# Joining attention's product with v into the scores' step, planning by a ring of four PSUM buffers, and dealing the weight preparation anew, in a kernel of attention and two MLPs

## The chip, the cores and the metric

The kernel runs on one core of a Trainium2 chip. The metric is the device time of one execution in microseconds (us).

## The reference

```python
def sm_attn(qq, kk, vv):
    s = scale * np.matmul(qq, kk.transpose(0, 1, 3, 2))
    s = s - np.max(s, axis=-1, keepdims=True)
    a = np.exp(s)
    a = a / (np.sum(a, axis=-1, keepdims=True) + 1e-09)
    return np.matmul(a, vv)
p_packed = sm_attn(p, k, v)            # 32 rows of p for each of 8 x 8 heads; q, k, v: 576 x 64 a head
out = sm_attn(q, p_packed, p_packed)
x = out.transpose(0, 2, 1, 3).reshape(4608, 512)
h = x @ w_in;   x = (h * sigmoid(h)) @ w_out              # MLP 1: 512 -> 2048 -> 512
h = x @ w_in2;  out = (h * clip(h + 3, 0, 6) / 6) @ w_out2   # MLP 2, the same sizes
```

All is fp32. The kernel gets its precision on TensorE (PE) by splitting each operand into a high and a low part (gh and gl, for example) and multiplying three times.

## The kernel before

**Blocks.** The 4608 rows of x are dealt into nine blocks of 512. Block j (0 to 7) holds the first 512 positions of batch j, block 8 the last 64 positions of all. MLP 1 runs over the blocks in order. A block goes through 16 slices f of the 2048 hidden units: `hidden` (L899 to L901) puts a 128 x 512 tile hps into PSUM, ACT takes silu of it (L907) and the high part gh (L914), DVE the low part gl (L915), and `project` (L922 to L924) multiplies it into four accumulators acc two slices later. In blocks 1 to 7 attention's second product is folded into MLP 1: packed values times w_in (`fuse_steps`, L660 to L662, written M here) give the tiles named fused, xf, xh, xl or raw, which `hidden` multiplies with the attention weights a2h and a2l; a slice then has 6 matmuls for hidden (written H) and 12 for project (P), against 12 and 12 in blocks 0 and 8. From about 823 us on the second MLP runs, which the change does not touch.

**Attention between the matmuls.** Heads come in groups of four, numbered n = 0 to 15 (two for each batch). Blocks 0 to 6 carry the attention of later blocks as short interruptions of PE's stream. One window of attention works on three groups at once: the first softmax of one (c, p against k), the second of another (d, q against the packed values), and what follows for two earlier ones (b and a). Its steps are

- `step_kpq` (L404 to L413): transposes of group b's softmax weights (d in the trace; ACT copies them into a T buffer at L108, DVE copies the tail a1Tt at L111), of p, and of the 64-position tails kt and qt;
- `step_tr` (L432 to L438): transposes of q and k rows into T buffers, by PE and ACT for n below 4, by DVE alone (L438) from n = 4 on;
- `products_pp` (L464, L467): group b's weights times v, the packed values; then pt (L486) and xt (L596), two single transposes;
- `step_zs` (L506 to L519): the scores of d (z) and c (s), each a 512-wide bank, and one bank `rest` for all 64-wide tails;
- `exps`: the exponentials on ACT (L449, L548), each with a change of the activation table before it and another for the silu behind it; `ends`: row sums and the division on DVE (L454, L455, L554 to L557).

All of these, and the M products, take their PSUM from one pool of four buffers (abank); hps comes from another tag of the same kind. A buffer that is asked for while its last reader has not finished stops PE.

**What sets the order.** The program of each engine is fixed in advance by `Plan`. Its clock `now` counts 512-wide matmuls. A step stands in a list with a place in the block, a cost, the steps that it needs, and a wait in matmuls after each of them, from the table WAIT (FIRST in block 0); it runs at the first `tick` at which its place is reached, its waits are over, a T buffer is free (`held`, four of them) and, if it asks for PSUM, its entry of `banks` (two release times) has passed. `exps` runs only right behind a slice's gh and gl.

**Loads.** `use` hands out the loads of later groups on SP's queue: tails of v and q, two v pieces, eight q and eight k pieces for a group from n = 4 on (L356, L366, L373).

**Preparation.** `Prep` turns the second MLP's weights into seven pieces in two precisions: 32 units of nine steps (two loads praw, conversions on ACT at L180, L186, L332 and L333, on DVE and on GpSimd, three stores). `nxt` calls `prep.step` once a slice in blocks 1 to 6, three times in block 7 and four times in block 8 after the first slices. In block 8 the second MLP's first x pieces are loaded as well.

## Time and profile before

| | us |
|---|---|
| median of 3 runs (1526.87 to 1527.33) | 1526.9 |
| the profiled execution | 1522.9 |
| its span | 1521.0 |
| PE busy in it | 1481.4 |
| block 0 begins | 35.7 |
| blocks 1, 2, 3, 4 begin | 151.2, 251.1, 340.4, 418.6 |
| blocks 5, 6, 7, 8 begin | 506.0, 588.1, 667.1, 732.6 |
| second MLP begins | 823.0 |

The profile has a row for each instruction: engine, line, operation, output and input tile, start and duration, and the idle time before it with the engine or transfer that ended it. The views used below are the page's busy times, the waits of one engine summed by who released them, the timeline of one engine, and windows (busy time of every engine, granted clock of PE and DMA rate in a stretch).

### The profile page before, as it was taken

To read this page: it belongs to the slowest core of one execution; us is meant where nothing else is said; L and a number is where in the kernel's file an instruction comes from. 1 tells how busy PE (TensorE), PEld (TensorE's weight loads), DVE (VectorE), ACT (ScalarE), POOL (GpSimd) and SP (SyncE) were. 2 spreads that over 40 slices of the span, in tenths; PEclk is the share of its full clock that TensorE was granted. 3 is DMA by queue.
4 is the path that set the end of the run, shared out by engine and by line. 5 is a ranking of instruction groups with operands and counts; after the bars stand their busy time and mean duration, and the time that the engine had idled before them with its cause. 6 is when DMAs were issued, how large, how long until landed. Compare 5 with 4: busy or idle time off the path is not lost.

```text
span 1521.0 us, 21714 instructions
## 1 busy us (share of the span) xinstructions
PE 1481.4 (97%) x7550; PEld 1227.8 (81%) x7550; DVE 1038.6 (68%) x1695; ACT 779.7 (51%) x1241; POOL 193.8 (13%) x177
## 2 busy tenths in 40 slices
PE   7999998999999999999999999999999999999998
PEld 4767766777777777788878888888888888999998
DVE  6767466655676556753543769776978687778777
ACT  6876656555666456564443344433443344444443
POOL 2433112111211211122231000000000000000000
PEclk9999999999999999999999999999999999999999
DMA  9998789897798768868696667577767766898987
GB/s 247 313 319 266 231 235 266 243 237 193 187 253 231 201 169 271 234 177 224 216 303 202 193 214 226 193 221 241 225 195 220 237 219 209 285 314 252 276 271 221
DMA packets 434508, 358.51 MB, mean 236 GB/s; under 512 B 191200, under 2 KB 325856, under 8 KB 434400
## 3 DMA queue, kind: packets, MB, share of 16 engines
q1 hardware_dynamic: 423632, 343.79, 77.3%
q10 hardware_dynamic: 10768, 13.34, 2.7%
q8 instruction: 61, 1.00, 0.3%
q14 instruction: 47, 0.39, 0.1%
HBM read 295.17 MB, written 61.87 MB: 235 GB/s over the span
## 4 chain that ended last, share of the span: by engine, by line
PE 83%; DVE 4%; ACT 4%; DMA 3%; SPq 2%; issue 1%; POOL 1%; ACTq 0%; DVEq 0%; POOLq 0%
PE b L1174 8%; PE b L1175 8%; PE b L1173 8%; PE b L1268 8%; PE b L1271 7%; PE b L1270 7%; PE acc L922 7%; PE acc L923 7%; PE acc L924 7%; PE hps L899 4%; PE hps L901 4%; PE hps L900 4%; SPq L373 1%; DMA w1i<-win 1%; PE abank L660 1%
## 5 line engine op out<-in xcount | busy, mean ns | idle before, releaser
L915 DVE TENSOR_TENSOR gl<-hps,gh 128x512 fp32r<-128x512 f32 x144 | 98.8, 686 | 157.6 <-ACT gh L914 157.1
L1270 PE MATMUL b<-ro,ws 128*128 128x512 f32 (+2 forms) x564 | 206.3, 366 | 0.0
L1271 PE MATMUL b<-ro,ws 128*128 128x512 f32 (+2 forms) x564 | 206.2, 366 | 0.0
L1173 PE MATMUL b<-xc,ws 128*128 128x512 f32 (+1 forms) x560 | 205.6, 367 | 0.0
L1175 PE MATMUL b<-xc,ws 128*128 128x512 f32 (+1 forms) x560 | 205.6, 367 | 0.0
L1174 PE MATMUL b<-xc,ws 128*128 128x512 f32 (+1 forms) x560 | 205.6, 367 | 0.0
L1216 DVE TENSOR_TENSOR ro<-g,ro 128x1024 fp32r<-128x1024 f32 (+1 forms) x140 | 161.1, 1155 | 42.3 <-ACT ro L1211 41.9
L1211 ACT CAST ro<-g 128x1024 fp32r<-128x1024 f32 (+1 forms) x140 | 132.1, 967 | 93.9 <-DVE g L1204 33.3
L1268 PE MATMUL b<-ro,ws 128*128 128x512 f32 (+2 forms) x564 | 139.0, 367 | 0.3
L907 ACT ACTIVATE hps<-hps 128x512 f32<-128x512 f32 x144 | 84.2, 585 | 86.4 <-PE hps L901 85.6
L922 PE MATMUL acc<-gh,wr 128*128 128x512 f32 x288 | 115.7, 402 | 1.7 <-ACT gh L914 1.7
L1270 PEld LDWEIGHTS b<-ro,ws 128*128 128x128 f32 x564 | 105.9, 188 | 13.2
L1271 PEld LDWEIGHTS b<-ro,ws 128*128 128x128 f32 x564 | 105.9, 188 | 13.1
L1173 PEld LDWEIGHTS b<-xc,ws 128*128 128x128 f32 x560 | 105.1, 188 | 13.3
L1174 PEld LDWEIGHTS b<-xc,ws 128*128 128x128 f32 x560 | 105.1, 188 | 13.2
L1175 PEld LDWEIGHTS b<-xc,ws 128*128 128x128 f32 x560 | 105.1, 188 | 12.9
L1268 PEld LDWEIGHTS b<-ro,ws 128*128 128x128 f32 x564 | 102.9, 188 | 15.0 <-DVE ro L1216 2.1
L922 PE MATMUL acc<-gh,wo 128*128 128x512 f32 x288 | 114.4, 397 | 0.0
L923 PE MATMUL acc<-gl,wr 128*128 128x512 f32 x288 | 113.4, 394 | 0.2 <-DVE gl L915 0.2
L924 PE MATMUL acc<-gh,wr 128*128 128x512 f32 x288 | 113.1, 393 | 0.0
L923 PE MATMUL acc<-gl,wo 128*128 128x512 f32 x288 | 112.4, 390 | 0.5 <-DVE gl L915 0.5
L924 PE MATMUL acc<-gh,wo 128*128 128x512 f32 x288 | 112.4, 390 | 0.0
(310 smaller groups left out, 2892.6 us busy)
## 6 DMA issues: line engine op xcount, KB each, us to landing
ws<-w2in SPq DMA_DIRECT2D x280, 256.0 KB, 3.4
ws<-w2out SPq DMA_DIRECT2D x280, 256.0 KB, 3.4
wi<-w1i SPq DMA_DIRECT2D x80, 512.0 KB, 5.9
wo<-w1o SPq DMA_DIRECT2D x64, 512.0 KB, 5.8
x1d<-x SPq DMA_DIRECT2D x18, 512.0 KB, 5.6
w1i<-win SPq DMA_DIRECT2D x16, 512.0 KB, 7.4
praw<-in_moe_w_in_dram SPq DMA_DIRECT2D x32, 256.0 KB, 5.8
praw<-in_moe_w_out_dram SPq DMA_DIRECT2D x32, 256.0 KB, 6.2
```

The lines of the kernel that those rows point to most:

```text
L915: nc.vector.tensor_sub(out=gl, in0=g, in1=f32(gh))
L922: mm(acc[e], lhsT=w[:, 0, s], rhs=gh, start=first, stop=False)
L923: mm(acc[e], lhsT=w[:, 0, s], rhs=gl, start=False, stop=False)
L924: mm(acc[e], lhsT=w[:, 1, s], rhs=gh, start=False, stop=last)
L1173: mm(ps, lhsT=wh, rhs=xs[k][:, 0, c], start=first, stop=False, skip_group_check=True)
L1174: mm(ps, lhsT=wh, rhs=xs[k][:, 1, c], start=False, stop=False, skip_group_check=True)
L1175: mm(ps, lhsT=wl, rhs=xs[k][:, 0, c], start=False, stop=last, skip_group_check=True)
L1211: nc.scalar.copy(out=t[:, 0], in_=v)
L1216: nc.vector.tensor_sub(out=t[:, 1], in0=self.operand(s), in1=f32(t[:, 0]))
L1268: mm(to, lhsT=wh, rhs=x, start=False, stop=last, skip_group_check=True)
L1270: mm(to, lhsT=wh, rhs=x, start=first, stop=False, skip_group_check=True)
L1271: mm(to, lhsT=wl, rhs=x, start=False, stop=False, skip_group_check=True)
```

## The change

1. From block 2 on, `products_pp` of group b and the transposes pt and xt are done inside `step_zs`, in free columns of its bank `rest`; pt and xt of a group that just finished go into the next `step_kpq` (arguments p and x). Block 1 keeps `products_pp` as a step of its own.
2. `Plan` keeps four release times (`ring`) in place of two, puts `hidden`'s tile into it as well, and asks that the next one does not come free later than the next hidden tile will want it. M products hold 15 in place of 11, T buffers are five in place of four, and the table of waits is different, with one for block 1 (SECOND): the exponentials wait longer after the scores, and the transposes longer after the exponentials. The transposes of k and q (`turn`) no longer stand behind `step_kpq` and pp.
3. `Prep`'s scratch buffer pr is one in place of two; block 7 does five steps a slice (78 in all, 46 before), block 8 two (32, 62 before). The loads of the second MLP's first x pieces go out one at a time in place of eight together.

The matmuls themselves are the same: PE has 6164 rows of instructions in place of 6165.

```diff
-            return self.pool.tile([P, T], F32, tag="pring", name="pr", bufs=2)
+            return self.pool.tile([P, T], F32, tag="pring", name="pr")
...
-    def step_kpq(c, d, b):
+    def step_kpq(c, d, b, p=None, x=None):
...
+        if p is not None:
+            step_pt(p)
+        if x is not None:
+            step_xt(x, ps[:, 3 * P:])
...
-            st["a1", b] = half_kb(b, "T", 4)
+            st["a1", b] = half_kb(b, "T", 5)
...
-    def products_pp(n):
+    def products_pp(n, ps=None):
         vm, vt = [nat.pop(("v", n, j)) for j in range(2)], nat.pop(("v", n))
         a, at_ = st.pop(("a1", n)), st.pop(("a1t", n))
-        ps = bank()
+        ps = bank() if ps is None else ps
...
-    def step_zs(c, d, b, a):
+    def step_zs(c, d, b, a, p=None):
...
         if b is not None:
-            step_pt(b, rest[:, P:2 * P])
+            products_pp(b, rest[:, 2 * TAIL:3 * TAIL])
+        if p is not None:
+            step_pt(p, rest[:, 3 * TAIL:5 * TAIL])
         if a is not None:
-            step_xt(a, rest[:, 2 * P:3 * P])
+            step_xt(a, rest[:, 5 * TAIL:7 * TAIL])
         if d is not None:
...
         if b is not None:
-            step_ptc(b)
+            st["pp", b] = value_pp(b, rest[:, 2 * TAIL:3 * TAIL])
+        if p is not None:
+            step_ptc(p)
...
-            self.steps, self.open, self.done, self.tiles, self.banks = [], set(), {}, [], [0, 0]
+            self.steps, self.open, self.done, self.tiles, self.ring = [], set(), {}, [], [0] * 4
+            self.hidden = self.period = 0
...
-            return tile and len(self.tiles) > 3 and self.tiles[-4] in self.open
+            return tile and len(self.tiles) > 4 and self.tiles[-5] in self.open
+
+        def take(self, hold):
+            self.ring = self.ring[1:] + [max(self.now, self.late) + hold * self.slow]
...
-            if bank and self.banks[count == 3] > self.now:
+            if bank and (max(self.ring[:count]) > self.now or self.slow > 1 and self.ring[count] > max(self.now, self.hidden + self.period)):
...
-                self.banks = [self.banks[1], max(self.now, self.late) + bank * self.slow]
+                self.take(bank)
...
+        def turn():
+            add(d, "q0", 0, lambda: step_tr(d, "q", 0), bank=0, tile=("z", d))
+            add(d, "q1", 0, lambda: [step_tr(d, "q", 1), use("q", d)], ("q0", d), bank=0, tile=("z", d))
+            add(a, "u", 0, lambda: [step_u(a), step_ut(a)], before[1], bank=8)
+            add(c, "k0", 0, lambda: step_tr(c, "k", 0), (("q1", d), 0), bank=0, tile=("s", c))
+            add(c, "k1", 0, lambda: [step_tr(c, "k", 1), use("k", c)], ("k0", c), bank=0, tile=("s", c))
...
+            p = pend.pop() if pend else None
+            p0, p1 = (p, None) if p is not None and p == d else (None, p)
...
+            def transposes():
+                step_kpq(c, d, b, p0, x)
...
+                add(keys[0][1], keys[0][0], 2 * n_banks, transposes, before[0] if b is not None else ("spread", c), ("spread", c), ("pp", p0), tile=b is not None and ("pp", b),
+                    bank=8, count=n_banks, also=keys[1:])
...
+            b0 = b if j > 1 else None
+            if j == 1:
+                add(b, "pp", 4, lambda: step_pp(b), ("t", b), ("tt", b))
+                p1 = b
+            turn()
+
+            def scores():
+                step_zs(c, d, b0, a, p1)
...
+                add(keys[0][1], keys[0][0], (5 if d is not None else 0) + (5 if c is not None else 0) + (4 if b0 is not None else 0) + 1, scores,
+                    ("pt", d), ("q0", d), ("q1", d), (("u", a), 0), ("k1", c), ("kpq", either), ("t", b), ("tt", b), ("pp", p1), ("u", a),
+                    bank=9, also=keys[1:], count=n_banks)
+            if b0 is not None:
+                if c is None and d is None and j + 1 in mates:
+                    add(b, "pt", 1, lambda: alone(b, step_pt, step_ptc), ("pp", b))
+                else:
+                    pend.append(b)
...
-    WAIT = {"spread": 8, "kpq": 7, "q0": 6, "q1": 6, "k0": 6, "k1": 6, "t": 6, "tt": 5, "pp": 9, "pt": 6, "z": 4, "zt": 10, "s": 4, "st": 7,
-            "exps": 18, "ends": 18, "u": 14, "split": 10, "xt": 12}
-    FIRST = {**WAIT, "ends": 16, "u": 26, "spread": 20, "exps": 14, "pt": 14, "pp": 24, "tt": 8, "t": 8, "k1": 8}
+    WAIT = {"spread": 8, "kpq": 7, "q0": 6, "q1": 8, "k0": 6, "k1": 8, "t": 8, "tt": 8, "pp": 9, "pt": 6, "z": 4, "zt": 10, "s": 4, "st": 7,
+            "exps": 22, "ends": 18, "u": 14, "split": 10, "xt": 12}
+    SECOND = {**WAIT, "exps": 19, "t": 6, "tt": 6}
+    FIRST = {**WAIT, "ends": 16, "u": 26, "spread": 20, "exps": 15, "pt": 14, "pp": 24, "tt": 8, "t": 8, "k1": 8}
...
+        plan.hidden, plan.period = plan.now, 3 * (len(parts) + KC)
+        plan.take(3 * len(parts) + 11)
...
                     load(k, half, side, c)
-                    if n:
-                        yield
-            if not n:
-                yield
+                    yield
...
-                    plan.add(("m", j, g, i), lo + (hi - lo) * 0.7 * (i + 0.5) / len(fs), 6 if len(mates[j]) == 1 else 3, fn, bank=11)
+                    plan.add(("m", j, g, i), lo + (hi - lo) * 0.7 * (i + 0.5) / len(fs), 6 if len(mates[j]) == 1 else 3, fn, bank=15)
...
-                plan.add(("m", j + 1, 0, i), lo + (0.99 - lo) * (i + 0.5) / len(fs), 6 if len(mates[j + 1]) == 1 else 3, fn,
-                         [(("split", j + 1, i * QPB // len(fs)), 10)], bank=11)
+                plan.add(("m", j + 1, 0, i), lo + (0.95 - lo) * (i + 0.5) / len(fs), 6 if len(mates[j + 1]) == 1 else 3, fn,
+                         [(("split", j + 1, i * QPB // len(fs)), 10), (("pp", mates[j + 1][-1] * QPB + QPB - 1), 0)], bank=15)
...
-                if j >= B - 1 or full:
+                for _ in range(1 + full if j == B - 1 else full):
                     prep.step()```

On ACT in block 1, around the exponentials of n = 6 and the copy T of their transposes, before:

```order
L914 CAST gh<-hps 128x512
L449 ACT_TABLE_LOAD
L449 ACTIVATE d_2330,s1m<-d_2330,s1m 128x576
L548 ACTIVATE d_145<-d_145 128x576
L332 CAST hi_2190<-c_2189 128x256
L333 CAST hi_2190<-c_2189 128x640
L108 COPY T<-abank 128x512
L108 COPY kp<-abank 128x256
L907 ACT_TABLE_LOAD
L907 ACTIVATE hps<-hps 128x512
```

and after (L457 and L560 are the exponentials, L959 the silu, L966 gh):

```order
L966 CAST gh<-hps 128x512
L457 ACT_TABLE_LOAD
L457 ACTIVATE d_2306,s1m<-d_2306,s1m 128x576
L560 ACTIVATE d_145<-d_145 128x576
L332 CAST hi_2250<-c_2249 128x256
L333 CAST hi_2250<-c_2249 128x640
L959 ACT_TABLE_LOAD
L959 ACTIVATE hps<-hps 128x512
L966 CAST gh<-hps 128x512
L108 COPY T<-abank 128x512
```

The table load, silu and gh of the next slice now stand between the exponentials and the copy of their transposes.

On DVE at the same window, before (L454 to L557 are the row sums and the division, L438 the transposes of k and q of the next scores):

```order
L454 TENSOR_SCALAR r_2434<-s1m 128x1
L455 RECIPROCAL r_2434<-r_2434 128x1
L554 TENSOR_REDUCE s2s<-d_145 128x18
L555 TENSOR_SCALAR s2s<-s2s 128x18
L556 RECIPROCAL s2s<-s2s 128x18
L557 TENSOR_TENSOR d_145<-d_145,s2s 128x576
L111 COPY a1Tt<-abank 64x128
L111 COPY qtT<-abank 128x128
L438 STREAM_TRANSPOSE T<-nat 128x512
L915 TENSOR_TENSOR gl<-hps,gh 128x512
L438 STREAM_TRANSPOSE T<-nat 128x512
```

and after (L446 are the transposes, L967 is gl):

```order
L446 STREAM_TRANSPOSE T<-nat 128x512 x4
L967 TENSOR_TENSOR gl<-hps,gh 128x512
L462 TENSOR_SCALAR r_2454<-s1m 128x1
L463 RECIPROCAL r_2454<-r_2454 128x1
L566 TENSOR_REDUCE s2s<-d_145 128x18
L567 TENSOR_SCALAR s2s<-s2s 128x18
L568 RECIPROCAL s2s<-s2s 128x18
L569 TENSOR_TENSOR d_145<-d_145,s2s 128x576
L111 COPY a1Tt<-abank 64x128
L111 COPY qtT<-abank 128x128
```

All four transposes and a gl now stand ahead of the sums, the division and a1Tt.

On PE in block 2, where an M product (L660) follows xt (L596) and hidden's matmuls, before:

```order
L596 MATMUL abank<-tails,ppf 128x128
L899 MATMUL hps<-a2h,fused 128x512
...
L901 MATMUL hps<-a2h,fused 128x512
L660 MATMUL abank<-wi,ph 128x512
L661 MATMUL abank<-wi,ph 128x512
L662 MATMUL abank<-wi,pl 128x512
L409 MATMUL abank<-ident,pbd 128x128
L413 MATMUL abank<-ident,kt 128x64 x2
```

and after (L608 is xt, L951 to L953 hidden, L672 to L674 M, L974 to L976 project):

```order
L608 MATMUL abank<-tails,ppf 128x128
L413 MATMUL abank<-ident,pbd 128x128
L417 MATMUL abank<-ident,kt 128x64 x2
L417 MATMUL abank<-ident,qt 128x64 x2
L951 MATMUL hps<-a2h,fused 128x512
...
L976 MATMUL acc_2861<-gh,wr_609 128x512
L672 MATMUL abank<-wi,ph 128x512
L673 MATMUL abank<-wi,ph 128x512
L674 MATMUL abank<-wi,pl 128x512
```

The transposes of p and of the tails now come ahead of the M product, in the buffer beside xt's, and three matmuls of project as well.

## Rows read from the trace of the kernel before

**Rows 1.** Page, part 1: busy time, share of span and instructions of each engine.

```profile
PE 1481.4 (97%) x7550; PEld 1227.8 (81%) x7550; DVE 1038.6 (68%) x1695; ACT 779.7 (51%) x1241; POOL 193.8 (13%) x177
```

**Rows 2.** Waits of PE: waiting tile, releaser: total us, times, longest us.

```profile
PE hps L899 <- DVE gl L915: 4.2, 3, 2.1
PE abank L404 <- ACT d L449: 4.2, 4, 2.1
PE abank L660 <- issue: 4.2, 3, 1.9
PE hps L899 <- DVE raw L668: 2.3, 2, 1.2
...
PE abank L467 <- DVE a1Tt L111: 2.3, 1, 2.3
PE acc L922 <- ACT gh L914: 1.7, 1, 1.7
PE abank L432 <- ACT T L108: 1.5, 1, 1.5
PE abank L510 <- DVE T L438: 0.9, 1, 0.9
...
PE hps L901 <- DVE fused L668: 0.8, 1, 0.8
```

**Rows 3.** PE's timeline: start, duration, instruction, idle before it and its releaser.

```profile
99.91 0.50 PE L899 MATMUL hps<-xh,win 128*128 128x512 f32 x1 [2.11 <-DVE gl L915]
...
200.07 1.08 PE L506 MATMUL abank<-T,ppT 128*64 128x512 f32 x4
...
296.85 0.40 PE L899 MATMUL hps<-a2h,fused 128*128 128x512 f32 x1
...
297.99 0.39 PE L901 MATMUL hps<-a2h,fused 128*128 128x512 f32 x1
299.97 0.47 PE L660 MATMUL abank<-wi,ph 128*128 128x512 f32 x1 [1.59 <-issue]
```

**Rows 4.** Windows: length, busy of engines, PE clock, DMA share, GB/s.

```profile
101.44:104.85 3.41, 3.41 (x10) 2.65 (x9) 2.69 (x5) 2.38 (x6) 0.19 (x1) 0.50 1.08 394
239.40:250.00 10.60, 8.23 (x61) 6.12 (x50) 6.92 (x16) 3.68 (x9) 4.03 (x5) 1.00 0.90 250
541.76:545.17 3.41, 3.41 (x9) 2.24 (x7) 2.12 (x5) 2.10 (x3) 0.00 (x0) 0.50 0.54 163
```

**Rows 5.** ACT's timeline across the exponentials of n = 7 in block 1.

```profile
232.89 1.28 ACT L449 ACT_TABLE_LOAD   x1
...
235.54 0.57 ACT L666 CAST fused<-abank 64x512 fp32r<-64x512 f32 x1
...
236.72 0.59 ACT L108 COPY T<-abank 128x512 f32<-128x512 f32 x1
237.33 1.28 ACT L907 ACT_TABLE_LOAD   x1
...
239.24 0.59 ACT L914 CAST gh<-hps 128x512 fp32r<-128x512 f32 x1
```

**Rows 6.** DVE's timeline at the same place.

```profile
232.91 0.69 DVE L915 TENSOR_TENSOR gl<-hps,gh 128x512 fp32r<-128x512 f32 x1 [2.19 <-ACT gh L914]
...
239.35 0.73 DVE L554 TENSOR_REDUCE s2s<-d 128x18 f32<-128x576 f32 x1
...
240.63 0.92 DVE L557 TENSOR_TENSOR d<-d,s2s 128x576 f32<-128x576 f32 x1
```

**Rows 7.** SP's timeline: first load of the v, q, k group of n = 6, 7.

```profile
204.78 0.99 SPq L356 DMA_DIRECT2D vt<-in_v_dram  x1
```

**Rows 8.** DVE's timeline: last of the four k and q transposes of that group.

```profile
222.91 0.71 DVE L438 STREAM_TRANSPOSE T<-nat 128x512 f32<-128x512 f32 x1
```

**Rows 9.** ACT's timeline: a conversion of the preparation that waited for its load.

```profile
535.65 0.66 ACT L180 ACTIVATE pr<-praw 128x512 f32<-128x512 f32 x1 [4.52 <-DMA praw<-in_moe_w_in_dram]
```

**Rows 10.** Window inside block 8, columns as in rows 4.

```profile
750.00:800.00 50.00, 48.05 (x211) 39.24 (x210) 25.89 (x43) 24.75 (x40) 16.36 (x13) 1.00 1.08 305
```

More of the change, by code (lines that the diff above doesn't have):

```diff
@@ L428, in step_kpq @@
             st["qt", d] = t
+        if x is not None:
+            step_xtc(x)
     def turn_rows(ps, m):
@@ L442, in step_tr @@
         turn_rows(ps, m)
-        t = half_kb(n, "T", 4)
+        t = half_kb(n, "T", 5)
         copy(out=t, in_=ps)
@@ L804, in tile_pack_attention_two_mlps, with window @@
     plan = Plan()
-    def window(c, d, b, a, first):
+    def window(c, d, b, a, j, x):
         steps = []
@@ L840, in window @@
         add(c, "spread", 0, lambda: spread_p(c), ("kpq", b), bank=0)
-        if b is not None:
-            add(b, "t", 2 + (2 if c is not None else 0), kpq, before[0], ("spread", c), tile=("pp", b), bank=7, count=2,
-                also=[("tt", b), ("kpq", either)])
-        else:
-            add(either, "kpq", 2, kpq, ("spread", c), bank=7)
-        add(d, "q0", 0, lambda: step_tr(d, "q", 0), (("k1", b), 0), (("t", b), 0), bank=0, tile=("z", d))
-        add(d, "q1", 0, lambda: [step_tr(d, "q", 1), use("q", d)], ("q0", d), bank=0, tile=("z", d))
@@ L848, in window @@
-        add(b, "pp", 4, lambda: step_pp(b), ("t", b), ("tt", b))
-        add(a, "u", 0, lambda: [step_u(a), step_ut(a)], before[1], bank=8)
-        split_pt, split_xt = first or b == d, first
-        if split_pt:
-            add(b, "pt", 1, lambda: [alone(b, step_pt, step_ptc), use("v", b)], ("pp", b))
-        if split_xt:
-            add(a, "xt", 1, lambda: alone(a, step_xt, step_xtc), ("u", a))
-        add(c, "k0", 0, lambda: step_tr(c, "k", 0), (("pp", b), 0), (("q1", d), 0), bank=0, tile=("s", c))
@@ L856, in window @@
-        add(c, "k1", 0, lambda: [step_tr(c, "k", 1), use("k", c)], ("k0", c), bank=0, tile=("s", c))
-        pt_, xt_ = None if split_pt else b, None if split_xt else a
-        def zs():
-            step_zs(c, d, pt_, xt_)
-            if pt_ is not None:
-                use("v", b)
-        keys = [("z", d), ("zt", d), ("s", c), ("st", c), ("pt", pt_), ("xt", xt_)]
-        lead = next((k for k in keys if k[1] is not None), None)
-        if lead:
-            add(lead[1], lead[0], (5 if d is not None else 0) + (5 if c is not None else 0) + 1, zs, ("pt", d), ("q0", d), ("q1", d), (("u", a), 0),
-                ("k1", c), ("kpq", either), ("tt", b), ("pp", pt_), ("u", xt_), bank=9, also=[k for k in keys if k != lead], count=3 if c is not None and d is not None else 2)
+        def turn():
[4 more added lines that the diff above has]
+            add(c, "k1", 0, lambda: [step_tr(c, "k", 1), use("k", c)], ("k0", c), bank=0, tile=("s", c))
@@ L1784, in tile_pack_attention_two_mlps @@
         n = QPB * (j + 1) - 1
-        if 0 < j < B:
+        if 0 < j < B and not ws:
             order.append((("xt", n), 1, lambda n=n: [step_xt(n), step_xtc(n)], (), None, 5, (), 1))
@@ L1788, in tile_pack_attention_two_mlps @@
         for c, d in ws:
-            order += window(c, d, *last, j == 0)
+            order += window(c, d, *last, j, n if ws[0] == (c, d) and 0 < j < B else None)
             last = c, d
@@ L1794, in tile_pack_attention_two_mlps @@
             place = sofar / total * (ATT.get(j, 0.83) if j < B - 1 else 0.2)
-            plan.add(key, place, cost, fn, [k if isinstance(k[0], tuple) else (k, (WAIT if j else FIRST).get(k[0], 0)) for k in need], tile, held, also, count)
+            plan.add(key, place, cost, fn, [k if isinstance(k[0], tuple) else (k, (SECOND if j == 1 else WAIT if j else FIRST).get(k[0], 0)) for k in need], tile, held, also, count)
             if any(k[0] == "pt" for k in (key, *also)):
```

33 lines of the change are left out of this document (30 added, 3 removed).

## The prediction

> **What bounds the kernel now.** I read the page's busy times first: PE is busy 1481.4 of the span's 1521.0 us [rows 1]. The change takes away no matmul, so only PE's idle time and its clock can move: 39.6 us of idle time in all, with the prologue and the second MLP in it. The view of PE's waits says who ends the rest [rows 2]: hidden's first matmul waits for the gl that releases its buffer, transposes of attention for the exponentials, M products and hidden for PSUM (written "issue") or for their fused or raw tiles. PE's timeline shows one wait of a kind at its place [rows 3]. A wait costs a little more than its idle time: from the matmul at 297.99 to the one at 299.97 are 1.98 us, a step is (297.99 - 296.85) / 5 = 0.228 us, so 1.75 us are lost where 1.59 us are shown as idle [rows 3]. I add 0.16 us to each.
>
> The windows give the second cost [rows 4]: for 3.41 us from 101.44 on and from 541.76 on the granted clock is 0.50, the lower of its two levels. Each time PE had just waited 2.1 us (the longest of two rows in [rows 2], one at 99.91 in [rows 3]). At half the clock a half of the 3.41 us is lost, 1.7 us each. Behind the 2.3 us wait for a1Tt (block 1, near 239) the window has the full clock [rows 4]: a wait of that length does not always bring a dip.
>
> **What the change removes.** I follow the new order of PE, DVE and ACT and ask of each wait whether what it waited for now has more time.
>
> - Block 0: hidden's waits for gl at 99.91 and one more (2 of 3, 4.2 less some 1.2 for the one that stays = 3.0); two of the four waits for the exponentials, some 1.2 of 4.2; the wait of the k transposes for a T copy, 1.5 [rows 2]. With 0.16 for each of the five: 3.0 + 1.2 + 1.5 + 0.8 = 6.5 us. They go because the new list never asks for a buffer whose release is near, and because exponentials stand one slice earlier than the transposes of their result.
> - Block 1: zs's wait for T 0.9, pp's for a1Tt 2.3, hidden's for fused 0.8 and one of the two for raw, 1.2 [rows 2]; with 0.6: 5.8. At the border to block 2 some 0.3 stay: 5.5 us.
> - Blocks 2 to 6: the three M waits 4.2, the other two waits for exponentials 3.0 (4.2 - 1.2), the other wait for raw 1.1 [rows 2]; with 1.0: 9.3 us. The longest of them hangs on the preparation: ACT stood 4.52 us at a conversion that waited for its load [rows 9], with silu and the exponentials behind it. In the new order that conversion stands behind the exponentials.
> - Block 8: project's wait for gh, 1.7 + 0.16 = 1.9 us [rows 2]. It too is a silu that stood behind a late conversion, in the stretch where the DMA engines are full (share 1.08, 305 GB/s, PE busy 48.05 of 50) [rows 10]. The change takes half of the preparation's steps out of this block.
>
> Together 6.5 + 5.5 + 9.3 + 1.9 = 23.2 us. The two dips go with their waits: 3.4 us.
>
> **What it adds in block 1.** Here pp is still a step of its own, six matmuls behind the transposes of the weights. The copy T and the tail a1Tt, which pp multiplies, used to follow the exponentials directly; now a table load, silu, gh and gl of the next slice stand ahead of them, and on DVE the division. For n = 6, from the end of hidden's last matmul ahead of the exponentials: silu and gh 1.4 (0.2 to start, then twice 0.59); table load and both exponentials 235.54 - 232.89 = 2.65; two conversions of the preparation some 1.0; load, silu and gh 239.24 + 0.59 - 237.33 = 2.5 [rows 5]; gl 0.7; sums and division 240.63 + 0.92 - 239.35 = 2.2 and two short ones 0.3; a1Tt 0.3 [rows 6]. Sum 11.1 us. PE's stream up to pp's tail: 27 matmuls x 0.228 = 6.2, the transposes some 1.15, pp's first part 0.5: 7.8 us. So pp waits 3.3 us. By the same steps n = 4 waits 1.7, n = 5 0.5, n = 7 2.9: 8.4 us.
>
> Two of these windows have more ahead of a1Tt: three (n = 5) and four (n = 6) transposes of q and k, which wait for loads on SP, and gl behind them. The group of loads took from 204.78 [rows 7] to the last transpose at 222.91 [rows 8], 18.1 us. In the new order, if SP begins the group when PE begins the scores ahead of it, the last transpose ends 18.1 + 0.7 later; gl, sums, division and a1Tt add 3.5: 22.3 us. PE's stream from those scores to pp's tail: 2.2 (scores and pt), 51 x 0.228 = 11.6, transposes 1.15, six matmuls 1.4, 0.5: 16.8 us. So n = 6 waits 5.5 us in place of 3.3. The same for n = 5, with one k and no division: 3.2 in place of 0.5. Block 1 adds 1.7 + 3.2 + 5.5 + 2.9 = 13.3 us. This is the least certain term. Below, 4 us, if ACT and DVE catch up (each wait of PE gives them time at the next); above, the loads start later: in the trace PE began those scores at 200.07 [rows 3] and SP the group at 204.78 [rows 7], 4.7 us behind. Twice 4.7 is 9.4 more. I take no delay, since SP's queue ahead of the group holds mostly w_in loads that wait for M products now placed earlier.
>
> Here the trace speaks against a page. Behind the table load at 237.33 silu and gh are done by 239.83: 2.5 = 1.28 + 2 x 0.59 and nothing else [rows 5]. The Trainium skill, "ScalarE: Activation LUTs", section "What ACT_TABLE_LOAD costs", says that a switch also takes a drain of 1380 ns, 2.66 us in all. By the page each of block 1's four waits would be some 1.4 us longer, 5.5 us together; by the row nothing, and the sum goes by the row.
>
> **What it adds elsewhere.** In blocks 2 to 6 pp comes with the next scores, 17 or more matmuls behind the transposes, or four in two cases a block; by the same chain n = 13 waits 1.2 and some others 0.1 to 0.2: 1.8 us (0 to 4). That copies of the tails now wait for pp in the same bank lengthens the chain to the exponentials by less than 1 us; the longer wait in the table covers it. Block 7 does five preparation steps a slice: a unit every 7.4 us in place of 12.3, each with a load that ACT waits for. Nothing of M or attention is left in that block, and gh has more than a slice until project wants it; I count 0.5 us. If the DMA engines fill there as in block 8, the price is that stretch's: 1.95 us idle in 50 [rows 10], 2.7 us for 70. The one scratch buffer in place of two is hidden, since its two uses lie five or more steps apart.
>
> **Sum.** -23.2 - 3.4 + 13.3 + 1.8 + 0.5 = -11.0 us. The profiled execution is 1522.9 us and would become 1511.9; the median of the runs is 1526.9, so 1515.9, rounded to 1516.
>
> **Rivals.**
> (a) Faster yet: block 1's new waits come to 4 us, since PE's first wait gives ACT and DVE the time that they lack later: -23.2 - 3.4 + 4 + 0.5 = -22.1, 1505 us. For it: one wait was chained by hand as if no other had come before. Against it: T and a1Tt stand behind the same rows in every window.
> (b) Slower: the loads of k and q decide. DVE's transposes stand ahead of gl, division and a1Tt; if SP begins both groups L us later than I assume, both pp wait L longer. With waits over 2 us PE may also dip twice, 3.4 us. It is slower by 0.2% from 2 L + 3.4 = 11.0 + 3.1 on, L = 5.3 us. The trace has 4.7 (see above); with 6 us, a delay that the preparation's loads on the same queue could bring: -11.0 + 12 + 3.4 = +4.4, 1531 us.
> (c) No change: L between 2 and 5, or waits that come back elsewhere because the ring of four is a guess of when buffers come free: some 1526 us. For it: most of the waits are 1 to 2 us, and a plan that moves one can make another. Against it: in the new order far fewer products ask for a buffer whose last reader has just begun.
> (d) Dips in place of dips: each of block 1's waits over 2 us (n = 5, 6, 7) is followed by a dip, 3 x 1.7 = 5.1 us: 1521 us. The rows bear it out twice and speak against it once [rows 4]. The Trainium skill, "TensorE: Matmul & The Clock Gate", section "Why this matters for your kernels", says that idle gaps between bursts of matmuls bring PE back to the lower clock; it would count these dips.
>
> **How the numbers follow.** Forecast, 1509 to 1519 us: 0.45. (a) 0.18, (d) 0.13, (c) 0.11, (b) 0.13. The forecast, (a) and (d) are faster by over 0.2% (3.1 us, about what a measurement of this kernel can tell from no change): 0.76; (c) is the same, 0.11; (b) slower, 0.13. The range leaves out a half of (a) and most of (b): from 1504 (block 1 at 4 us, all else as summed) to 1529 (L = 4.7 in both groups with both dips: -11.0 + 9.4 + 3.4 = +1.8).
>
> **What would show it.** Right: no M product waits at "issue" in blocks 2 to 6; no wait of the transposes for the exponentials; no hidden waits for gl at block 0's end; no clock of 0.50 near 100 and 540; PE waits for T or a1Tt only at pp in block 1, 13 us together, with DVE idle at L446 for a k load; blocks 2 to 6 shorter by some 9 us, block 8 by 2. Wrong: DVE idle at L446 for 8 us or more with PE at project's gl behind it; conversions in block 7 that wait over 6 us and a gh that PE waits for; new waits at zs because the joined pp wants a1Tt.

## The result, and the profile after

| | before | after |
|---|---|---|
| median (lowest to highest), 8 runs each, us | 1527.1 (1524.4 to 1530.0) | 1536.5 (1529.9 to 1541.6) |
| the profiled execution, us | 1522.9 | 1529.9 |
| its span, us | 1521.0 | 1528.1 |

The ratio is 1.0058 [1.0038, 1.0077]: slower by 0.6%, where 1516 us and a gain of 0.7% were forecast; the range ended at 1529. Both profiled executions are the shortest that were seen of their kernel, and their spans differ by 7.1 us. PE has 7550 instructions in both profiles.

The windows view gives a table by stage (length; busy time of PE, PEld, DVE, ACT and POOL with instructions; granted clock of PE; DMA share; GB/s). The rows are block 0, block 1, blocks 2 to 6, block 7 and block 8. Before:

```profile
35.65:151.22 115.57, 108.61 (x574) 84.08 (x572) 82.41 (x149) 86.30 (x161) 46.00 (x38) 0.99 0.98 299
151.22:251.11 99.89, 95.76 (x589) 72.24 (x588) 57.44 (x125) 57.54 (x96) 14.73 (x17) 1.00 0.84 230
251.11:667.09 415.98, 405.69 (x2149) 317.68 (x2148) 271.14 (x540) 248.41 (x419) 68.81 (x67) 1.00 0.80 222
667.09:732.64 65.55, 65.55 (x291) 54.30 (x290) 25.31 (x53) 34.62 (x60) 20.10 (x17) 1.00 0.74 200
732.64:823.02 90.38, 87.97 (x386) 71.94 (x384) 40.09 (x67) 39.87 (x65) 25.04 (x18) 1.00 0.92 263
```

After:

```profile
36.26:150.45 114.19, 107.45 (x574) 83.12 (x572) 84.58 (x152) 86.86 (x161) 45.85 (x38) 1.00 0.98 305
150.45:258.64 108.19, 95.93 (x589) 73.12 (x588) 55.74 (x123) 57.45 (x96) 13.99 (x17) 0.98 0.80 216
258.64:667.21 408.57, 402.67 (x2150) 317.60 (x2148) 265.88 (x539) 247.19 (x418) 68.20 (x67) 1.00 0.79 223
667.21:743.13 75.92, 70.23 (x291) 54.80 (x290) 33.17 (x73) 42.14 (x74) 32.43 (x27) 0.98 0.92 249
743.13:830.20 87.07, 87.07 (x385) 72.07 (x384) 32.64 (x48) 32.38 (x51) 11.26 (x8) 1.00 0.71 213
```

The first number behind each stretch is its length: block 0 loses 1.4 us, block 1 gains 8.3, blocks 2 to 6 lose 7.4, block 7 gains 10.4, block 8 loses 3.3; with 0.6 ahead of block 0 the span grows by 7.1. In block 7 before, PE was busy for the whole 65.55 us; now it is busy 70.23 of 75.92, and 1.7 us of the busy time is what a stretch at half clock cost.

PE's waits after, beside [rows 2]:

```profile
PE abank L475 <- DVE a1Tt L111: 10.9, 5, 4.5
...
PE acc L974 <- ACT gh L966: 4.6, 4, 2.6
PE abank L672 <- DMA wi<-w1i: 3.0, 2, 1.6
PE abank L472 <- ACT T L108: 2.1, 3, 1.3
PE abank L608 <- DVE xf L680: 1.8, 1, 1.8
...
PE abank L404 <- ACT d L457: 1.5, 1, 1.5
PE hps L951 <- DVE raw L680: 1.4, 2, 0.7
```

Hidden's waits for gl (4.2 us) have become one of 1.1, M's waits at "issue" (4.2) two of 1.0 in all, the transposes' for the exponentials (4.2) one of 1.5. In their place stand pp's wait for the tail a1Tt (L475, 10.9 us) and for T (L472, 2.1), project's for gh (L974, 4.6), M's for a w_in load (3.0) and xt's for a buffer (L608, 1.8).

The dips (stretches at half clock) at 101 and 541 [rows 4] are gone; two others have come, one at pp's longest wait in block 1, one at gh's longest in block 7:

```profile
196.37:199.78 3.41, 3.20 (x15) 2.45 (x16) 1.62 (x5) 1.50 (x3) 0.00 (x0) 0.50 0.87 298
739.09:742.50 3.41, 3.41 (x9) 2.64 (x10) 3.38 (x5) 3.35 (x6) 1.62 (x1) 0.50 0.68 185
```

**The rest of the gap** is in part clock. The median of the granted clock over the span is 0.9915 for the changed kernel (8 runs) and 0.994 for the kernel before (29 runs); the profiled executions have 0.996 and 0.997. At half clock one half of the time is lost, so 0.001 of the mean is 0.001 x 1528 = 1.5 us where PE is busy: of the 9.5 us between the medians at most 3.8 are clock, the rest waits. One more trace shows a place for it: the run with the old dealing (the first experiment below) has the changed kernel's program up to block 7, and there block 1 takes 113.9 us in place of 108.2, with the same waits at pp (12.7 us in place of 12.3) and three dips of 3.4, 6.8 and 6.8 us in place of one of 3.4.

### The profile page after: what moved, and what is told of

Read it like the earlier page. It is cut to its first block, busy times and chain, and to the rows that moved or that the text cites. A ratio compares the mean times of both kernels' runs of the same rounds, so it can differ in the third digit from the quotient of the medians.

```text
span 1528.1 us, 21726 instructions
## 1 busy us (share of the span) xinstructions
PE 1482.3 (97%) x7550; PEld 1229.2 (80%) x7550; DVE 1034.6 (68%) x1695; ACT 778.8 (51%) x1241; POOL 190.8 (12%) x177
## 4 chain that ended last, share of the span: by engine, by line
PE 81%; DMA 6%; DVE 4%; ACT 4%; SPq 2%; issue 1%; POOL 1%; ACTq 0%; POOLq 0%; DVEq 0%
PE b L1223 8%; PE b L1224 8%; PE b L1222 8%; PE b L1317 7%; PE b L1320 7%; PE b L1319 7%; PE acc L974 7%; PE acc L975 7%; PE acc L976 7%; PE hps L951 4%; PE hps L953 4%; PE hps L952 4%; DMA nat<-in_k_dram 1%; DMA w1i<-win 1%; DMA wi<-w1i 1%
## 5 line engine op out<-in xcount | busy, mean ns | idle before, releaser
L967 DVE TENSOR_TENSOR gl<-hps,gh 128x512 fp32r<-128x512 f32 x144 | 98.8, 686 | 173.8 <-ACT gh L966 173.4
L959 ACT ACTIVATE hps<-hps 128x512 f32<-128x512 f32 x144 | 84.2, 584 | 99.7 <-PE hps L953 98.9
L974 PE MATMUL acc<-gh,wo 128*128 128x512 f32 x288 | 116.1, 403 | 2.8 <-ACT gh L966 2.8
L974 PE MATMUL acc<-gh,wr 128*128 128x512 f32 x288 | 113.7, 395 | 1.8 <-ACT gh L966 1.8
L976 PE MATMUL acc<-gh,wo 128*128 128x512 f32 x288 | 113.4, 394 | 0.0
L976 PE MATMUL acc<-gh,wr 128*128 128x512 f32 x288 | 112.4, 390 | 0.0
```

The costliest lines, as they stand in the source:

```text
L967: nc.vector.tensor_sub(out=gl, in0=g, in1=f32(gh))
L974: mm(acc[e], lhsT=w[:, 0, s], rhs=gh, start=first, stop=False)
L976: mm(acc[e], lhsT=w[:, 1, s], rhs=gh, start=False, stop=last)
```

## Experiments

The changed kernel's parts are undone one at a time, or put into the kernel before. Medians are of 4 to 12 runs, each beside runs of the kernel before on the same chip; its own medians there were 1527.1 to 1529.3, so ratios are to be compared.

### The dealing of the preparation

Undone in the changed kernel:

```diff
-                for _ in range(1 + full if j == B - 1 else full):
+                if j >= B - 1 or full:
                     prep.step()
```

> The changed kernel with one part undone: the preparation is dealt to blocks 7 and 8 as before the change (46 and 62 steps in place of 78 and 32). Changed kernel: block 7 takes 75.9 us (before 65.6), block 8 87.1 (before 90.4). Theory A (the dealing itself makes block 7 long: five steps a slice put ACT's waits for praw, for GpSimd's sums and for DVE's pieces ahead of silu and gh): block 7 back to 66, block 8 to about 90, the whole 7 us shorter than the changed kernel, about 1529 to 1530, ratio to the kernel before about 1.001. Rival B (the scratch buffer, now one in place of two, is what makes the conversions late): block 7 stays near 76 or falls by a third only, ratio 1.004 to 1.006.

1526.9 us, ratio 0.9996 [0.9984, 1.0009]. Block 7 takes 65.6 us, block 8 89.2: theory A. 9.6 us of the median hang on this one line, and the scratch buffer is still single. In the seven traces with three or four steps a slice block 7 takes 65.55 us, in the six with five steps and the units themselves unchanged 74.1 to 76.4. Put alone into the kernel before, the edit the other way round:

> The kernel before with the new dealing alone (blocks 7 and 8: 78 and 32 steps), two scratch buffers kept. Theory A (the dealing): block 7 grows from 65.6 to about 76, block 8 falls from 90.4 to about 87, the whole is 7 us longer: 1534, ratio 1.004 to 1.005. Rival B (one scratch buffer): block 7 stays at 66 to 68, and block 8 gains 3: ratio 0.998 to 1.000.

1539.6 us, ratio 1.0075 [1.006, 1.009]. Block 7 takes 76.4 us, with both scratch buffers: the dealing, not the buffer. Block 8 did not get shorter (93.3 us): there the eight x loads still go out at once, gl stood behind DVE's wait of 10.4 us for them, PE waited 3.1 us for gl and dipped. By these rows, what block 8 gained in the changed kernel needs the loads one at a time as well; no run changes those loads alone. ACT's waits in block 7 of this run are those of the changed kernel:

```profile
ACT hi L332 <- POOL c L324: 16.0, 8, 3.3
ACT pr L180 <- DMA praw<-in_moe_w_out_dram: 11.4, 4, 4.3
```

### Block 1: two causes

One number, 18 in place of 19, puts the copy T in front of the next silu again:

```diff
-    SECOND = {**WAIT, "exps": 19, "t": 6, "tt": 6}
+    SECOND = {**WAIT, "exps": 18, "t": 6, "tt": 6}
```

> The changed kernel with one number: in block 1 the transposes wait 18 in place of 19 after the exponentials. By the order of ACT this puts the copy T back in front of the next slice's table load, silu and gh, for all four groups; the four transposes of q and k of n = 6 stay ahead of a1Tt. Changed kernel: pp waits 1.4, 4.5, 3.3 and 3.1 us for n = 4 to 7 (12.3 together), block 1 takes 108.2 us (before 99.9). Theory A (T and a1Tt behind silu make the waits): n = 4 and n = 7 lose theirs, n = 5 falls to about 2, n = 6 stays near 3; waits of the transposes for the exponentials come back at about 0.7 each (3): block 1 about 104, the whole 4 us shorter than the changed kernel. Rival C (the loads of k make the waits, DVE's transposes standing ahead): n = 5 and n = 6 stay at 4.5 and 3.3, block 1 falls by 2 at most.

1529.7 us, ratio 1.0015 [1.0004, 1.0027]. The waits of n = 4, 5 and 7 are gone, as theory A has it; all that they had covered is now one wait at n = 6:

```profile
226.71 0.44 PE L475 MATMUL abank<-vt,a1Tt 64*32 64x64 f32 x8 [9.29 <-DVE a1Tt L111]
```

and PE then ran at half clock for three times the length of the usual dip, part of it while it waited:

```profile
220.99:231.23 10.24, 4.52 (x18) 3.49 (x19) 5.55 (x14) 2.82 (x4) 0.00 (x0) 0.50 0.92 254
```

So block 1 takes 107.0 us in this trace (an execution 4.9 us above the run's median): the loads decide n = 6. Moving DVE's transposes back behind the weights' and pp (PE's order stays the same):

```diff
-            add(d, "q0", 0, lambda: step_tr(d, "q", 0), bank=0, tile=("z", d))
+            add(d, "q0", 0, lambda: step_tr(d, "q", 0), *([(("t", b), 0)] if j == 1 else []), bank=0, tile=("z", d))
...
-            add(c, "k0", 0, lambda: step_tr(c, "k", 0), (("q1", d), 0), bank=0, tile=("s", c))
+            add(c, "k0", 0, lambda: step_tr(c, "k", 0), (("q1", d), 0), *([(("pp", b), 0)] if j == 1 else []), bank=0, tile=("s", c))
```

> The changed kernel with DVE's order changed at one place, PE's order the same: in block 1 the transposes of q stand behind the transposes of the weights, those of k behind pp, as before the change. Theory A (ACT's and DVE's chain from the exponentials makes pp's waits): n = 4, n = 6 and n = 7 stay at 1.4, 3 and 3.1, n = 5 falls from 4.5 to about 1; zs waits up to 1 us for its transposes: block 1 about 106, 2 us shorter. Rival C (loads of k): n = 5 and n = 6 both fall to under 1, the waits come back at zs only where a load is really late (1 to 2 us): block 1 about 103, 5 us shorter.

1530.6 us, ratio 1.0019 [1.0007, 1.0031]. The wait of n = 5 is gone, those of n = 4, 6 and 7 stay at 1.1, 2.6 and 3.1: theory A for these three, the load for n = 5, and zs did not wait at all. Block 1 takes 106.3 us in this trace (an execution 2.1 us above the run's median), 4.7 of them lost in two dips. Both edits together:

> Both edits of block 1 together: the transposes wait 18 in place of 19 after the exponentials (T ahead of the next silu), and DVE's transposes of q and k stand behind the weights' transposes and pp again. Theory A + C (pp's waits have two causes, the chain behind silu and the late loads, and each edit left the other's): pp waits under 1.5 us in all for n = 4 to 7, the transposes for the exponentials up to 2 us, block 1 about 100 to 102 (changed kernel 108.2 in its trace, before 99.9); the whole 9 to 11 us shorter than the changed kernel's 1536.5, ratio to before 0.998 to 1.000. Rival (the waits move to zs: the transposes now come late for the scores): block 1 stays at 105 to 107.

1526.8 us, ratio 0.9986 [0.9973, 0.9999]. Block 1 takes 100.5 us, no pp waits in it. One new wait of 2.7 us, of project for a wo load behind a group of loads on SP, came with a dip.

By the waits at pp the two causes partly hide behind each other: the edits take 3.0 and 5.2 us of the 12.3 alone and 12.1 together. By the ratios no hiding shows: against the changed kernel's 1.0058 the edits alone bring 6.6 and 6.0 us, both together 11.0, each within some 3 us. Each alone is worth more than the block's length in its trace lets appear. With the old dealing besides:

> The same with the preparation dealt as before the change. If the losses of block 1 and of block 7 are all that stands against the change's gains, they add: block 7 back to 66, block 8 at 89, block 1 at 100 to 102, the whole about 1517, ratio 0.993 to 0.995, faster than both kernels. If the clock dips come back elsewhere (a wait of 2 us is left), about 1521, ratio 0.996.

1517.8 us, ratio 0.9929 [0.991, 0.9947]: faster than both kernels, as the sum of the parts says. Its windows (block 1, blocks 2 to 6, block 7, block 8):

```profile
150.58:251.41 100.83, 96.91 (x589) 73.30 (x588) 57.71 (x125) 58.18 (x97) 14.06 (x17) 0.98 0.84 223
251.41:663.06 411.65, 404.30 (x2150) 318.82 (x2148) 265.45 (x537) 246.62 (x417) 68.14 (x67) 1.00 0.80 225
663.06:728.61 65.55, 65.55 (x291) 54.29 (x290) 26.45 (x54) 34.62 (x60) 20.10 (x17) 1.00 0.74 200
728.61:816.59 87.98, 87.71 (x385) 71.86 (x384) 41.79 (x67) 39.77 (x65) 23.04 (x18) 1.00 0.95 271
```

Four preparation steps a slice in block 7 and three in block 8, on the same base, counted by `calls[0]`:

```diff
-                if j >= B - 1 or full:
+                calls[0] += 1
+                for _ in range(1 + (calls[0] % 3 == 1) if j == B - 1 else calls[0] % 4 != 0 if j == B else full):
                     prep.step()
```

> Both edits of block 1, and four preparation steps a slice in block 7 and three in block 8 (five and two in the changed kernel, three and four before the change). If ACT's waits in block 7 grow steadily with the rate: block 7 about 69 to 70, block 8 about 88, 2 to 3 us longer than with three and four. If the waits only reach project beyond a threshold (gh has about a slice of time): block 7 at 65.6, block 8 at 87.5 to 88, 1 to 2 us shorter.

1517.7 us, ratio 0.9929 [0.9914, 0.9944]. Blocks 7 and 8 take 65.6 and 87.0 us in its trace: a threshold between four and five. At four steps a slice ACT's waits reach nobody, at five they cost 10 us. The microsecond that block 8 gained cannot be seen in the median.

### What the join itself brings

```diff
-            b0 = b if j > 1 else None
-            if j == 1:
+            b0 = None
+            if j >= 1:
                 add(b, "pp", 4, lambda: step_pp(b), ("t", b), ("tt", b))
```

> As the run with both edits of block 1 and the old dealing, but pp is a step of its own in every block, as in block 1, and pt comes with the scores: the join alone undone, the ring, the tables and the five T buffers kept. Blocks 2 to 6 take 89.2, 78.2, 87.4, 82.1, 79.0 us before the change (415.9) and 86.3, 78.0, 86.9, 78.0, 79.4 after (408.6). Theory J (the join brings this): blocks 2 to 6 lose 4 to 7 us again, in waits of pp for T or a1Tt. Theory R (the ring and the waits bring it, the join is free of effect): blocks 2 to 6 stay within 1.5 us of 408.6.

1527.4 us, ratio 0.9988 [0.9976, 1.0001]: 0.6% or 9 us behind the same kernel with the join. Blocks 2 to 6 take 418.3 us (411.6 with it), a dip of 1.7 us among them in both: theory J. The waits at pp are back, here in block 5:

```profile
543.71 0.65 PE L472 MATMUL abank<-nat,T 128*32 128x64 f32 x32 [0.87 <-ACT T L108]
546.36 0.32 PE L475 MATMUL abank<-vt,a1Tt 64*32 64x64 f32 x8 [1.99 <-DVE a1Tt L111]
```

So the change's first part brings some 9 us. The order of block 1 and the dealing cost twice that, 1.29% or some 20 us from the changed kernel to the one with both mended, and what is left when all three are undone (the ring, the tables, five T buffers, one scratch buffer, the x loads one at a time) is 0.1% faster than the kernel before, within the noise. Taken to block 1 too (`b0 = b if j >= 1`, with the number 19, q and k ahead, and four and three steps):

> The join taken to block 1 as well (pp with the next scores there too), the waits of the changed kernel (19), q and k transposes ahead as in the changed kernel, four and three preparation steps a slice in blocks 7 and 8. Theory A (pp waits in block 1 because it stands six matmuls behind the transposes): no wait at pp for T or a1Tt in block 1, and it needs neither of the two edits there: block 1 at 99 to 102, ratio 0.993 like the kernel with both edits and this dealing. Rival C (the late loads of k hold DVE and with it the whole block): the waits move to zs and to project's gl, 5 us or more, block 1 at 104 to 108, ratio 0.996 to 0.999.

1521.9 us, ratio 0.9963 [0.9949, 0.9976]. The ratio is rival C's; block 1 takes 110.7 us, longer than either forecast. The waits moved not to zs and project but to the transposes and to pt, by what DVE has queued behind its k transposes (fused, gl), which stood at L446 for loads of q and k:

```profile
218.35 0.42 PE L407 MATMUL abank<-ident,d 128*64 128x128 f32 x1 [5.39 <-DVE fused L680]
221.06 0.48 PE L494 MATMUL abank<-ident,ppf 128*128 128x128 f32 x1 [2.29 <-DVE gl L967]
```

n = 7 still waits at pp, 1.3 and 1.9 us: the last window of the block has nothing else to join it to.

### Which of ACT's waits makes block 7 long

The load of the next unit two steps earlier (its expectation says three):

> The changed kernel with the preparation's load of the next unit three steps earlier (behind the first conversion in place of behind the third step), five steps a slice in block 7 kept. There ACT waited 10.9 us for praw, 16.0 for GpSimd's c and 8.0 for DVE's c in blocks 7 and 8 together. Theory L (the load is late by its lead of six steps): waits for praw nearly gone, PE's waits for gh in block 7 (4.6 us and a dip) fall to under 1.5, block 7 from 75.9 to 67 to 69. Theory G (the steps stand too close for GpSimd and DVE, whatever the load): the waits for c stay or grow, block 7 stays at 73 to 76.

1540.8 us, ratio 1.0099 [1.0078, 1.0121], block 7 78.1 us. It does not tell the theories apart: SP issued the loads a median of 1.1 us behind the start of the conversion, against 1.7 in the changed kernel, since the stores of the unit before stand ahead of them on its queue, and ACT still waited 12.5 us for praw in block 7. Two runs that each move one of the waits: hi one step later (a `yield` more ahead of it, one fewer behind),

> The changed kernel with ACT's conversion hi of the preparation one step later than DVE's sums (and one empty step fewer behind it), five steps a slice in block 7 kept. There ACT waited 16.0 us for GpSimd's c, 5.2 for DVE's c and 10.9 for praw. Theory G (hi stands too close behind GpSimd and DVE): waits for c fall from 21 to under 12 us, PE's waits for gh fall, block 7 from 75.9 to 69 to 72. Theory L (the loads set the pace: whatever ACT does not wait for at hi it waits for at praw): waits for praw grow by as much, block 7 stays at 74 to 77.

1537.5 us, ratio 1.0055 [1.0025, 1.0086]: the median did not move. Block 7 takes 72.7 us. ACT's waits in it for GpSimd's c fell from 16.0 to 13.7 us, those for praw rose from 10.9 to 12.6, as theory L has it; but PE's waits for gh fell from 4.6 to 2.5 us, and the block is shorter than L allows:

```profile
ACT hi L333 <- POOL c L324: 13.7, 8, 2.2
ACT pr L180 <- DMA praw<-in_moe_w_out_dram: 12.6, 6, 4.1
```

and loads two units ahead (`praw` three buffers, `hi7` one):

> The changed kernel with the preparation's loads two units ahead in place of one (three praw buffers, and one hi buffer to make room), five steps a slice in block 7 kept. Theory L (the loads are late): waits for praw in block 7 fall from 10.9 to under 3 us and block 7 from 75.9 to 67 to 71. Theory G (the chain of GpSimd, DVE and ACT within a unit): waits for GpSimd's c stay at 16, block 7 stays at 73 to 76; the single hi buffer may add waits of ACT for a store.

1536.1 us, ratio 1.0056 [1.0034, 1.0078]. Block 7 takes 69.0 us: its waits for praw are gone, and the single hi buffer brings waits for a store:

```profile
ACT hi L333 <- DMA w2out<-hi: 13.0, 3, 5.4
ACT hi L333 <- POOL c L325: 10.7, 5, 3.3
```

Both theories hold a part: by block 7's length the loads account for 6.9 of the 10.4 us (5.1 against the 74.1 us of the run with both edits of block 1, where block 7 has no dip either), the place of hi for 3.2, each by one trace. In the second kernel a wait of ACT of 5.1 us for a store of hi took much of the gain back in block 5, where PE then waited 2.5 us and dipped; its median did not move.

### The k loads on another queue

```diff
-                    nc.sync.dma_start(out=g[o:o + NP], in_=rows[h]...
+                    (nc.gpsimd if what == "k" else nc.sync).dma_start(out=g[o:o + NP], in_=rows[h]...
```

> The changed kernel with the eight k pieces of each group issued by GpSimd's queue in place of SP's, the order of PE, DVE and ACT kept. In block 1 SP issues q's and k's sixteen pieces in a row, 0.67 us each. Theory C (SP's serial issue makes k late, DVE's transposes wait with a1Tt behind them): k lands up to 5 us earlier, pp's waits of n = 5 and n = 6 (4.5 and 3.3 us in the changed kernel) fall to about 1 and 2, those of n = 4 and 7 stay at 1.4 and 3.1; block 1 at 103 to 105 in place of 108.2, ratio 1.002. Rival G (GpSimd issues a piece of this shape more slowly than SP, over 1.4 us each, or waits itself behind the preparation's sums): k lands later, n = 5 and n = 6 wait 8 us or more, block 1 at 114 or longer, ratio over 1.01.

> The kernel with both edits of block 1 and four and three preparation steps a slice, and k's pieces on GpSimd's queue. There project waited 3.5 us near 249 for a wo load that stood behind a group of loads on SP, and an M product 3.1 us near 288 for a w_in load. Theory C: with eight pieces fewer ahead on SP the wo wait falls to under 1 us and the w_in wait to about 1: 3 to 6 us shorter, dips included, ratio 0.989 to 0.991 (0.993 without the edit). Rival G: GpSimd's issue is slower; DVE waits for k, and the preparation's sums on GpSimd are late: ratio 0.996 or more.

1705.6 and 1700.6 us, ratios 1.1171 [1.1151, 1.1191] and 1.113 [1.1113, 1.1146]: rival G, and far beyond its price in both. The line's view (instructions with shortest, median and longest duration in ns; idle time of the engine before them with its count) shows the 96 pieces on GpSimd:

```profile
L373 POOL DMA_DIRECT2D nat<-in_k_dram x96: 697/708/819, 97.2 to 700.0; - x96
...
  issue: 231.9, 79
```

0.71 us each, and 231.9 / 79 = 2.9 us of idle time before most, for which the profile shows no releaser ("issue"): some 3.6 us a piece, 29 us for a group of eight. GpSimd's sums for the weights stand behind them: ACT's hi alone waits 119.8 us for a sum. In the first of the two traces blocks 0 to 5 are 8 to 43 us longer than in the changed kernel, block 6 is not.

## Why the prediction was wrong

| term | forecast, us | by the two traces, us |
|---|---|---|
| block 0, with its dip | -8.2 | -1.4 |
| block 1: 5.5 removed, 13.3 added | +7.8 | +8.3 |
| blocks 2 to 6, with their dip | -9.2 | -7.4 |
| block 7 | +0.5 | +10.4 |
| block 8 | -1.9 | -3.3 |
| sum (0.6 ahead of block 0 in the trace) | -11.0 | +7.1 |
| more in the median execution (9.5 less 7.1) | 0 | +2.4 |

One sum of the prediction is off: rival (a) leaves out the 1.8 us of blocks 2 to 6. With it the sum is -20.3 us and the time 1506.6, and the lower end of the range moves there too; the result lies beyond the other end.

**Right: block 1, by its mechanism.** pp waited 1.4, 4.5, 3.3 and 3.1 us for n = 4 to 7, 12.3 together (13.3 forecast: 1.7, 3.2, 5.5, 2.9). That the sum is so near is in part luck: n = 5 was 1.3 us longer, n = 6 2.2 us shorter than forecast. PE's rows for n = 5 and n = 6, each the larger part of a wait:

```profile
196.58 0.44 PE L475 MATMUL abank<-vt,a1Tt 64*32 64x64 f32 x8 [4.49 <-DVE a1Tt L111]
...
225.30 0.32 PE L475 MATMUL abank<-vt,a1Tt 64*32 64x64 f32 x8 [2.71 <-DVE a1Tt L111]
```

and DVE's, which stood at L446 for the loads with gl, sums and a1Tt behind it, twice:

```profile
192.07 0.71 DVE L446 STREAM_TRANSPOSE T<-nat 128x512 f32<-128x512 f32 x1 [2.25 <-DMA nat<-in_q_dram]
194.80 0.71 DVE L446 STREAM_TRANSPOSE T<-nat 128x512 f32<-128x512 f32 x1 [2.03 <-DMA nat<-in_k_dram]
...
196.26 0.26 DVE L111 COPY a1Tt<-abank 64x128 f32<-64x128 f32 x1
...
219.34 0.71 DVE L446 STREAM_TRANSPOSE T<-nat 128x512 f32<-128x512 f32 x1 [1.26 <-DMA nat<-in_k_dram]
221.56 0.71 DVE L446 STREAM_TRANSPOSE T<-nat 128x512 f32<-128x512 f32 x1 [1.51 <-DMA nat<-in_k_dram]
222.19 0.65 DVE L967 TENSOR_TENSOR gl<-hps,gh 128x512 fp32r<-128x512 f32 x1
...
224.97 0.28 DVE L111 COPY a1Tt<-abank 64x128 f32<-64x128 f32 x1
```

The assumption that decided rival (b) held too: SP began the group of n = 6 at 204.43, when PE began the scores (204.64 in PE's rows):

```profile
204.43 0.62 SPq L356 DMA_DIRECT2D vt<-in_v_dram  x1
```

The transposes ended 17.8 us later (forecast 18.8). The drain that the Trainium skill, "ScalarE: Activation LUTs", section "What ACT_TABLE_LOAD costs", counts with a table load was rightly left out: with it the four waits would be 5.5 us longer than forecast, and they came out shorter. In the changed kernel's trace the next instruction starts 0.01 us behind 34 of the 36 table loads, and all begin within 0.02 us of the end of the instruction before.

**Near, but only in part for its reason: blocks 2 to 6.** The waits for the exponentials (3.0 us) and the dip went, as forecast. Of "the three M waits 4.2" 3.7 us are left, two waits for a w_in load (1.6 and 1.4) and one still at "issue" (0.7). The two waits for raw fell from 2.3 to 1.4. And two waits that were counted in block 1, for fused at 253.18 and for raw at 257.16, lie in block 2, which begins at 251.1: by their places block 1 was forecast at +9.8 and blocks 2 to 6 at -11.2 us. Waits and dip account for some 6.2 of the 7.4 us; the rest shows in no wait of the view.

**Wrong: block 7, 10 us.** The failed step is "gh has more than a slice until project wants it; I count 0.5 us". It counted ACT's wait for the load, once a unit. The trace of the changed kernel shows two kinds of wait, here over two units of ACT's rows, with silu and gh behind them:

```profile
722.40 0.66 ACT L180 ACTIVATE pr<-praw 128x512 f32<-128x512 f32 x1 [4.02 <-DMA praw<-in_moe_w_out_dram]
...
727.97 0.41 ACT L332 CAST hi<-c 128x256 fp32r<-128x256 f32 x1 [2.15 <-POOL c L324]
...
735.25 0.41 ACT L332 CAST hi<-c 128x256 fp32r<-128x256 f32 x1 [3.26 <-POOL c L324]
...
736.94 0.58 ACT L959 ACTIVATE hps<-hps 128x512 f32<-128x512 f32 x1
737.55 0.58 ACT L966 CAST gh<-hps 128x512 fp32r<-128x512 f32 x1
```

The conversion waited 4.0 us for its load, hi 2.15 and 3.26 us for GpSimd's sum. Before the change a unit had 12.3 us, and ACT mostly found the sum ready; at 7.4 us the steps meet the sums (1.3 us on GpSimd, then four of 0.3 us on DVE) while these run. In block 7 ACT's waits for GpSimd's c went from 0.7 to 16.0 us, those for praw from 0.6 to 10.9; those for DVE's part of c hardly changed (6.2 and 5.2). The sum itself was late in part because silu was: GpSimd waited for L199 on DVE, which stands behind gl and so behind gh (gl ran from 732.03 on):

```profile
733.91 1.31 POOL L324 TENSOR_TENSOR c<-pr,praw 128x512 int32<-128x512 int32 x1 [2.49 <-DVE pr L199]
```

project then came late, and a dip followed:

```profile
738.19 0.50 PE L974 MATMUL acc<-gh,wo 128*128 128x512 f32 x1 [2.62 <-ACT gh L966]
```

I had also bounded the price by the wrong rows: block 8's stretch with full DMA engines shows what a late load costs at up to four steps a slice, not what five steps cost. The sign of being wrong that the prediction gave, late conversions in block 7 and a gh that PE waits for, is the one that came.

**Wrong: block 0, 7 us.** "They go because the new list never asks for a buffer whose release is near, and because exponentials stand one slice earlier": three of the five waits went, but the one at 109 grew, that at 113 stayed at half its size, and two came at new places:

```profile
73.78 0.66 PE L440 MATMUL abank<-ident,nat 128*128 128x128 f32 x4 [1.10 <-DVE gl L967]
...
109.05 0.66 PE L404 MATMUL abank<-ident,d 128*128 128x128 f32 x4 [1.47 <-ACT d L457]
...
113.59 0.66 PE L440 MATMUL abank<-ident,nat 128*128 128x128 f32 x4 [0.82 <-ACT T L108]
...
132.33 0.49 PE L608 MATMUL abank<-tails,ppf 128*128 128x128 f32 x2 [1.84 <-DVE xf L680]
```

The k transposes wait for a buffer whose reader gl stands behind conversions on DVE, the exponentials ran late behind the weights' conversions on ACT (which had itself waited for a load), and xt waits for a buffer whose reader xf stands behind four conversions. In sum PE's waits in block 0 are what they were (6.9 us before, 6.7 after); what went is the dip. In block 0 ACT and DVE are each busy for some 85 of the 114 us, and a plan that counts in matmuls does not see that they run late. The order of the instructions tells who stands behind whom, not when; I had chained times by hand in block 1 only. This is read from the rows: no run here changes block 0 alone.

**Wrong: dips.** I counted two dips removed and none added, and gave new ones a chance of 0.13 as rival (d). In blocks 0 to 8 of the changed kernel's trace there are two, one of them in block 1, and the median of its clock says that most executions have more. In the trace with the old dealing block 1 has the three dips that rival (d) speaks of, and is 5.7 us longer for nearly the same waits.

## What to carry to other kernels

Deal background work by what the engine that runs it must wait for in between, not by its busy time: the preparation's steps cost nothing in block 7 at four a slice and 10 us at five, because every wait inside a step stands ahead of the slice's own silu. A step moved ahead on an in-order engine takes all that stands behind it along: a transpose that waits for a load holds gl, the division and the tail that PE wants. When a plan improves one part and loses by others, undo the parts one at a time and keep what pays: the join with the old dealing and two edits in block 1 is 0.7% faster than the kernel before.

## What the runs showed of the hardware

- **Waits and dips.** Over blocks 0 to 8 of 14 traces, all of them but the two with k on GpSimd's queue, every one of the 17 waits of PE of 2.76 us or more goes with a stretch at half clock, 25 of the 50 waits of 1.75 to 2.75 us do, and of the 161 of 0.6 to 1.75 us only four, each within 4 us of a longer one. The stretches last 3.41, 6.83 or 10.24 us; one of 3.41 us costs 1.7 us when PE is busy throughout. A wait of the same length at the same place brings a dip in one execution and not in the next: that of 2.7 us at 225 us in the changed kernel brought none, that of 2.6 us at 226 us in the run with loads two ahead did. This may be part of why runs of one kernel spread, by 12 us for the changed kernel's 8 and by 8 us for 29 of the kernel before; no run separates it.
- **A late load can show as a wait for something else.** No wait of PE in the changed kernel's block 1 names a load: PE waits for a1Tt and T, DVE waits for nat. In the run with the number 18 the wait for a1Tt is 9.3 us, and only DVE's rows at L446 tell that loads stand behind it (3.3 and 1.5 us for q, 2.3 and 1.8 for k).
- **A load on GpSimd's queue** took that engine some 3.6 us a piece of 64 KB, 0.7 of them busy and 2.9 idle, against 0.63 us on SP's (median of q's 96 pieces in the same run).

One more wait is left open: in the kernels with both edits of block 1 project waits for a wo load, and a dip comes with it:

```profile
245.84 0.76 PE L974 MATMUL acc<-gh,wo 128*128 128x512 f32 x1 [3.27 <-DMA wo<-w1o]
```

No run here moves that load alone.
